# The section ahead of the list in written order: w by two queues, the path's flag by a product with ones, the powers in a weights' buffer, and 14 dummy products on TensorE

## The chip, the cores and the metric

The kernel runs on one core of a Trainium2 chip. A time is the device time of one execution, in microseconds (us). The kernel before was run 9 times: the median is 514.84 us. One further execution was recorded by the hardware profiler; every duration below comes from that one. Engines are named as in the profile: PE is TensorE's matmul side (PEld its weight loads), DVE is VectorE, ACT is ScalarE, POOL is GpSimd and SP is SyncE, which here only issues DMA transfers.

## What is computed

The kernel computes a linear attention with a decaying state, and a feed-forward block on its output, all in float32 (the four weights come as float64 words and are converted in the kernel). B = 4, H = 8, S = 768, D = 48; d_ff = 1024.

```python
for t in range(S):
    kt, vt, rt = (k[:, :, t], v[:, :, t], r[:, :, t])
    cur = np.einsum('bhd,bhe->bhde', u[None] * kt, vt)
    y[:, :, t] = np.einsum('bhd,bhde->bhe', rt, state + cur)
    state = w[None, :, :, None] * state + np.einsum('bhd,bhe->bhde', kt, vt)
x = np.ascontiguousarray(y.transpose(0, 2, 1, 3)).reshape(B * S, H * D)
a = x @ w1
b = x @ w2
out = (a * b @ w3) @ w_out
```

## The kernel before

**Units and the list.** A unit is one chunk of 128 tokens of one batch entry: 6 chunks by 4 entries, 24 units, numbered n. Almost all work is given by a list written out by hand, ORDER, of words such as `d.0` or `a.0.3.2`. `listed()` (line 745) runs through it under `manual_schedule`, so each of PE, ACT, DVE and SP does its instructions in the order of the list. The words that matter here:

- `kr.n`, `v.n` (`load`, line 197): load k and r, or v, of unit n, on SP. k and r go to `krin`, three buffers by n mod 3; v to `vnat`.
- `W.i` (`fetch`, line 218): load weights piece i on SP into `raws[i % 3]`. `M.i`, `N.i`, `H.i`, `L.i`, `Q.i` (lines 327 to 357) convert it on ACT, DVE, DVE, ACT and DVE.
- `d.n`, `e.n`, `f.n` (lines 399 to 408, DVE): r times k into the tile `ruk`, times u (the tile `ub`), and the sum by head. `g.n` (line 410, ACT) places it on diagonals.
- `k.n` (`scale`, line 388, DVE): k and r times the powers of w (`pn`), into `krs`.
- `U.n` (line 498, PE): products for the state. `T.n`, `R.n` (line 436, PE): transposes of `krs`. `A.n` (line 508), `S.n` (line 597) and `V.n` (line 616): the attention's products on PE. `i.n`, `j.n` (line 515, DVE): the state. `m.n` (line 539, DVE): the mask.
- `a`, `b`, `c`, `u` (lines 646 to 663): the products with w1 and w2; `G`, `K`, `F`, `X` fold w3 and w_out into one matrix; `P`, `E`, `D` are the last product and the stores.

The order of the list isn't planned at run time: an instruction goes when it is at the head of its engine and its inputs and its buffer are there.

**The section ahead of the list** (lines 149 to 278) isn't under `manual_schedule`. It does these things:

- POOL makes the identity and the masks and clears the pads of buffers (lines 156 to 191). ACT warms its table with one activation (line 183).
- SP loads w as one row (`wrow`, line 227), w as two columns of 48 partitions (`wucol`, line 229), k and r of unit 0, weights piece 0, u (`ub`, line 232), v of unit 0, k and r of unit 1, weights piece 1 and v of unit 1, in this order (lines 225 to 237).
- DVE finds the smallest and the largest w from `wrow` and writes `flag`, one integer that says whether all of w lies within W_LOW = 0.6 and W_HIGH = 1.6 (lines 240 to 245).
- DVE makes the powers of w: limits it (line 252), squares it six times (line 254), takes reciprocals (line 255) and doubles its way up to 64 positions and their inverses in a tile `both` of its own (lines 258 to 269), and copies each half to its second half (line 271). PE transposes the 8 blocks (line 274) and ACT copies the two results to `pn_in` (line 275).
- Each engine loads `flag` (`values_load`, line 277) and takes the branch to `program(True)` or `program(False)` (line 835). With these inputs it is `program(True)`, the list; `program(False)` is a general path that isn't run.

The tile `both` is freed at the end of that section, and tiles of the list, `ruk` among them, are allotted from the room that it leaves.

Of the kernel before, what the change touches and what calls it, by code (L numbers as in the profile page):

```python
# [23 lines left out]
M.1 h.1 j.0 S.0 t.1 d.2 R.1 k.2 m.0 r.1 R.2 kr.5 e.2 U.1 N.1 r.2 f.2 A.1 M.2 H.1 T.2 i.1 L.1 m.1 V.0 d.3 p.1 W.4 Q.1
v.3 Y.0 t.2 j.1 S.1 g.2 N.2 A.2 k.3 V.1 H.2 R.3 kr.6 Y.1 U.2 m.2 M.3 v.4 T.3 N.3 L.2 a.0.0.0 k.4 r.3 W.5 i.2 a.0.1.0
H.3 p.2 c.0.0.0 e.3 L.3 R.4 j.2 S.2 f.3 M.4 W.6 U.3 Q.3 b.0.0.0 o.4 h.3 c.0.1.0 i.3 t.3 V.2 d.4 p.3 k.5 kr.7 T.4 Y.2
e.4 A.3 v.5 r.4 x.5 S.3 t.4 b.0.1.0 m.3 o.5 y.5 j.3 M.5 V.3 u.0.0.0 u.0.1.0 U.4 f.4 Y.3 v.6 A.4 Q.2 g.4 a.0.0.1 k.6
N.5 b.0.0.1 M.6 N.6 m.4 c.0.0.1 H.6 a.0.1.1 z.5 u.0.0.1 L.6 H.5 b.0.1.1 c.0.1.1 x.6 W.9 L.5 a.0.2.2 u.0.1.1 y.6 i.4
W.8 l.5 Q.6 p.4 d.5 a.0.3.2 Q.5 c.0.2.2 kr.8 j.4 N.4 e.5 S.4 H.4 c.0.3.2 M.8 z.6 U.5 f.5 M.9 V.4 N.8 d.6 L.4 A.5 i.5
kr.9 b.0.2.2 Y.4 h.5 o.6 e.6 W.7 p.5 m.5 v.7 l.6 Q.4 b.0.3.2 j.5 u.0.2.2 N.9 k.7 U.6 f.6 A.6 x.7 g.6 S.5 k.8 y.7 V.5  # L30
d.7 M.7 a.0.4.2 m.6 v.8 kr.10 o.7 e.7 u.0.3.2 Y.5 f.7 z.7 x.8 b.0.4.2 c.0.4.2 d.8 y.8 h.7 kr.11 e.8 i.6 a.0.5.2 f.8
p.6 u.0.4.2 l.7 d.9 j.6 b.0.5.2 c.0.5.2 e.9 H.8 f.9 L.8 H.9 W.11 d.10 L.9 A.7 Q.8 W.12 U.7 u.0.5.2 a.0.6.2 N.7 i.7 H.7
p.7 k.9 L.7 a.0.7.2 j.7 kr.12 c.0.6.2 x.9 W.10 Q.9 y.9 S.6 Q.7 c.0.7.2 z.8 o.8 V.6 m.7 e.10 b.0.6.2 Y.6 g.8 v.9 N.10
N.11 S.7 M.10 f.10 M.11 u.0.6.2 z.9 V.7 o.9 H.10 b.0.7.2 l.8 d.11 Y.7 H.11 v.10 L.10 e.11 L.11 Q.10 W.13 g.9 Q.11 W.14
a.1.0.2 N.12 u.0.7.2 M.12 f.11 H.12 M.13 a.1.1.2 d.12 L.12 N.13 e.12 c.1.0.2 W.15 Q.12 M.14 H.13 N.14 L.13 b.1.0.2
H.14 c.1.1.2 W.16 Q.13 L.14 Q.14 W.17 M.15 N.15 b.1.1.2 H.15 u.1.0.2 L.15 Q.15 W.18 M.16 N.16 A.8 H.16 u.1.1.2 a.1.2.2
L.16 m.8 l.9 W.19 N.17 M.17 Q.16 H.17 M.18 b.1.2.2 N.18 c.1.2.2 H.18 L.17 L.18 Q.17 W.20 M.19 Q.18 W.21 G.0.0 N.19
G.0.1 K.0.0 u.1.2.2 U.8 H.19 a.1.3.2 K.0.1 i.8 L.19 k.10 p.8 W.22 M.20 N.20 kr.13 x.10 F.0 c.1.3.2 H.20 M.21 y.10 j.8
L.20 Q.19 W.23 M.22 Q.20 N.21 N.22 H.21 H.22 L.21 b.1.3.2 X.0 Q.21 W.24 L.22 Q.22 W.25 M.23 N.23 A.9 u.1.3.2 U.9 H.23
S.8 i.9 L.23 z.10 V.8 k.11 o.10 a.1.4.2 g.10 N.24 x.11 v.11 kr.14 Q.23 Y.8 m.9 y.11 b.1.4.2 p.9 W.26 N.25 f.12 c.1.4.2  # L40
j.9 l.10 d.13 e.13 S.9 u.1.4.2 o.11 A.10 z.11 a.1.5.2 m.10 a.1.6.2 c.1.5.2 l.11 a.1.7.2 c.1.6.2 b.1.5.2 V.9 u.1.5.2
U.10 c.1.7.2 v.12 G.1.0 i.10 Y.9 G.1.1 g.11 k.12 b.1.6.2 x.12 kr.15 p.10 f.13 y.12 K.1.0 d.14 b.1.7.2 M.24 j.10 M.25
e.14 u.1.6.2 K.1.1 H.24 S.10 H.25 L.24 z.12 A.11 u.1.7.2 o.12 U.11 Q.24 L.25 V.10 m.11 W.28 G.2.0 k.13 g.12 W.27 G.2.1
v.13 F.1 i.11 kr.16 Q.25 p.11 f.14 N.26 Y.10 j.11 l.12 d.15 K.2.0 x.13 K.2.1 e.15 y.13 N.27 G.3.0 X.1 U.12 S.11 k.14
o.13 V.11 i.12 kr.17 A.12 Y.11 x.14 G.3.1 v.14 g.13 a.2.0.2 z.13 m.12 K.3.0 f.15 y.14 p.12 d.16 G.4.0 K.3.1 e.16
b.2.0.2 j.12 K.4.0 c.2.0.2 l.13 U.13 u.2.0.2 S.12 k.15 z.14 o.14 V.12 i.13 A.13 Y.12 x.15 G.4.1 g.14 v.15 F.2 m.13
y.15 kr.18 K.4.1 f.16 l.14 d.17 M.26 e.17 M.27 H.26 p.13 H.27 L.26 j.13 S.13 L.27 W.29 Q.26 M.28 W.30 V.13 Q.27 o.15
z.15 N.28 A.14 Y.13 H.28 U.14 X.2 m.14 G.5.0 L.28 v.16 G.5.1 i.14 g.15 F.3 W.31 Q.28 N.29 k.16 M.29 f.17 kr.19 p.14
H.29 j.14 L.29 x.16 l.15 Q.29 S.14 y.16 K.5.0 N.30 d.18 X.3 F.4 K.5.1 N.31 e.18 o.16 z.16 G.6.0 X.4 G.6.1 K.6.0 F.5
M.30 K.6.1 H.30 M.31 L.30 H.31 Q.30 L.31 s.1.2.0 Q.31 s.1.2.1 F.6 s.1.0.0 X.5 s.1.2.3 s.1.1.0 s.1.3.0 s.1.1.2 s.1.3.1  # L50
s.1.1.1 s.1.3.3 s.1.3.2 s.1.0.1 s.1.0.2 s.1.0.3 s.1.2.2 G.7.0 X.6 s.1.1.3 U.15 K.7.0 G.7.1 i.15 P.0.0.0 K.7.1 k.17
p.15 F.7 x.17 kr.20 j.15 y.17 A.15 X.7 s.0.1.0 V.14 s.0.0.0 E.0.0.0 l.16 B.0 P.0.1.0 Y.14 v.17 s.0.0.1 g.16 m.15
a.2.1.2 s.0.0.3 B.1 E.0.1.0 f.18 B.2 a.2.2.2 c.2.1.2 B.3 s.0.1.2 s.0.0.2 s.0.2.0 b.2.1.2 d.19 c.2.2.2 s.0.2.2 s.0.2.1
s.0.1.1 s.0.2.3 s.0.3.0 b.2.2.2 s.0.1.3 s.0.3.1 u.2.1.2 s.0.3.3 e.19 s.0.3.2 P.0.0.2 u.2.2.2 P.0.1.2 E.0.0.2 P.0.0.3
E.0.1.2 P.0.0.4 E.0.0.3 P.0.1.3 E.0.0.4 P.0.0.5 E.0.1.3 P.0.1.5 E.0.0.6 E.0.0.5 D.0.0.0 P.0.1.4 E.0.1.6 A.16 E.0.1.4
U.16 E.0.1.5 m.16 D.0.1.0 P.0.0.6 i.16 k.18 p.16 P.0.0.1 j.16 kr.21 S.15 x.18 z.17 o.17 V.15 E.0.0.1 E.0.0.7 U.17 Y.15
a.2.3.2 i.17 g.17 y.18 v.18 k.19 D.0.0.1 kr.22 p.17 f.19 a.2.4.2 l.17 d.20 j.17 c.2.3.2 x.19 e.20 y.19 P.0.1.1 c.2.4.2
# [34 lines left out]
def kernel(  # L92
# [139 lines left out]
    nc.sync.dma_start(out=ub.rearrange("t h d -> t (h d)"),  # L232
                      in_=u.rearrange("h d -> (h d)").rearrange("(o n) -> o n", o=1).to_broadcast([P, DM]))
# [12 lines left out]


    pn_in = const.tile([C, 2, H, PAD], F32)
    with tc.tile_pool(name="once", bufs=1) as once, tc.tile_pool(name="psW", bufs=2, space=PSUM) as psW:
# [9 lines left out]
        nc.vector.memset(both[:, 0, :, HT:HT + 1], 1.0)  # L259
        nc.vector.tensor_copy(out=both[:, 1, :, HT:HT + 1], in_=wn_in[:, 0, NP:2 * NP, :])  # L260
        bf = both.rearrange("x g p t -> x (g p) t")
        for l in range(LEVELS):
# [4 lines left out]
            nc.vector.tensor_mul(bf[:, :, HT - 2 * n + 1:HT - n + 1] if n < HT else bf[:, :, 0:1],
                                 bf[:, :, HT - n + 1:HT + 1] if n < HT else bf[:, :, HT:HT + 1],
                                 wn_in[:, l, 0:2 * NP, :].to_broadcast([P, 2 * NP, n if n < HT else 1]))
        for g in range(2):  # L270
            nc.vector.tensor_copy(out=both[:, g, :, T:], in_=both[:, g, :, :T])
            ps = psW.tile([P, NP, C], F32, tag="w", name=f"ps_p{g}")
            for p in range(NP):
                nc.tensor.transpose(ps[:, p, :], both[:, g, p, :], ident)
# [594 lines left out]
```

## Time and profile before

| | |
|---|---|
| median of 9 runs | 514.84 us (513.56 to 517.12) |
| the profiled execution: its own time | 516.05 us |
| its span, first to last instruction | 514.2 us |
| granted TensorE clock, mean | 0.99 |
| busy: PE, PEld | 492.1 us (96%), 323.5 us (63%) |
| busy: DVE, ACT, POOL | 278.1 us (54%), 183.7 us (36%), 6.1 us (1%) |
| moved by DMA | 52.72 MB, mean 103 GB/s |
| landing after issue, median: k, r, v | 3.9, 4.3, 4.0 us |
| landing after issue, median: weights piece of 768 KB | 6.1 us |

How to read the profile's views: the page cuts the span into 40 slices of 12.9 us and gives the busy share of each engine in tenths, and the granted clock of TensorE in tenths of full speed. The chain of work that ended last is followed back from the last instruction, at each step to what released it; its lines give start, length and what ran. The timeline gives start, length, engine, line, operation and tiles, and in brackets how long the engine had been idle and what released it. For SP, a line is the issue of a DMA, and its length is the time that the issue took, not the transfer. A table of stages gives, for each stretch, the busy time of each engine, the granted clock and the DMA engines' share.

### The profile page before, as it was taken

The page shows a single profiled execution, that of the slowest core. Times are in us where ns is not written, and L with a number is a line of the kernel's source. Part 1 is how long each engine was busy: PE and PEld are TensorE (multiplying, and loading weights), DVE is VectorE, ACT ScalarE, POOL GpSimd, SP SyncE. Part 2 cuts the span into 40 slices and gives each one's busy share as a digit, 9 for nine tenths or more (in the row PEclk, how much of TensorE's full clock was granted, in tenths as well). Part 3 has the DMA queues.
Part 4 walks back from the last instruction along what each step waited for, and adds up shares of the span by engine and source line. Part 5 has one row for each costly group of instructions (what it writes and reads, how often), then busy time and mean ns, then how long its engine had stood idle before and what let it go on. Part 6 is the DMA issues. An engine that isn't in the chain of part 4 may idle for free.

```text
span 514.2 us, 12195 instructions
## 1 busy us (share of the span) xinstructions
PE 492.1 (96%) x5192; PEld 323.5 (63%) x5192; DVE 278.1 (54%) x587; ACT 183.7 (36%) x455; POOL 6.1 (1%) x23
## 2 busy tenths in 40 slices
PE   1889999999999899999999999999999999999996
...
PEclk9969999999999999999999999999999999999999
DMA  7988796668547781302601301230050100000001
GB/s 171 231 221 243 184 245 189 182 222 247 157 104 199 188 228 31 78 1 63 170 32 57 83 0 46 64 89 22 0 144 28 48 2 0 15 17 17 1 17 67
DMA packets 96865, 52.72 MB, mean 103 GB/s; under 512 B 77729, under 2 KB 88226, under 8 KB 96802
## 3 DMA queue, kind: packets, MB, share of 16 engines
...
q8 instruction: 43, 0.70, 0.6%
...
## 4 chain that ended last, share of the span: by engine, by line
PE 87%; DMA 6%; DVE 4%; issue 1%; ACT 1%; SPq 0%; DVEq 0%; ACTq 0%
PE ps_a L652 23%; PE ps_b L652 22%; PE ps_w L380 7%; PE ps_y L626 3%; PE ps_s4b L709 3%; PE ps_a11b L709 3%; PE ps_a22t L709 3%; PE ps_s2t L709 3%; PE ps_a12b L709 3%; PE ps_s1t L709 3%; PE ps_s3t L709 3%; PE ps_y L612 3%; PE ps_a L512 3%; PE ps_a L505 2%; DMA raw<-in_moe_w_dram 2%; DMA krin<-in_r_dram 1%
## 5 line engine op out<-in xcount | busy, mean ns | idle before, releaser
L652 PE MATMUL ps_a<-xT,w 128*128 128x512 f32 (+1 forms) x300 | 132.4, 585 | 0.0
L652 PE MATMUL ps_b<-xT,w 128*128 128x512 f32 (+1 forms) x300 | 130.9, 577 | 0.0
L652 PEld LDWEIGHTS ps_b<-xT,w 128*128 128x128 f32 x300 | 56.2, 190 | 62.0 <-issue 57.6
L663 DVE TENSOR_TENSOR abt<-ps_b,a 128x512 f32<-128x512 f32 (+1 forms) x50 | 33.3, 667 | 109.9 <-PE ps_b L652 109.9
L652 PEld LDWEIGHTS ps_a<-xT,w 128*128 128x128 f32 x300 | 56.1, 193 | 57.1 <-issue 53.6
L658 ACT COPY a<-ps_a 128x512 f32<-128x512 f32 (+1 forms) x50 | 28.3, 567 | 132.6 <-PE ps_a L652 128.0
L537 ACT COPY wide<-st 64x192 f32<-64x192 f32 x88 | 30.6, 347 | 59.4 <-DVE st L529 27.6
L380 PE MATMUL ps_w<-wo,w3T 128*128 128x384 f32 x128 | 42.5, 487 | 0.0
L419 ACT ACTIVATE AT<-same,dg 128x64 f32<-128x64 f32 x160 | 40.4, 336 | 5.5 <-DVE dg L408 3.0
L380 PEld LDWEIGHTS ps_w<-wo,w3T 128*128 128x128 f32 x128 | 23.9, 190 | 15.7 <-ACT wide L537 0.2
L354 ACT ACTIVATE t<-raw 128x512 uint32<-128x512 uint32 (+2 forms) x32 | 22.4, 706 | 7.7 <-DVE w3n L350 5.1
L626 PE MATMUL ps_y<-AT,vnat 64*64 64x64 f32 x1152 | 23.3, 226 | 1.2 <-issue 1.2
L540 DVE COPY_PREDICATED AT<-later,ps_a 128x512 f32<-128x512 int32 x24 | 17.5, 730 | 11.1 <-PE ps_a L505 7.0
L392 DVE TENSOR_TENSOR krs<-krin,pn_in 128x768 f32<-128x768 f32 x24 | 22.8, 949 | 0.1
L626 PEld LDWEIGHTS ps_y<-AT,vnat 64*64 64x64 f32 x1152 | 20.0, 138 | 4.4 <-issue 2.7
L505 PE MATMUL ps_a<-vnat,krs 64*64 64x48 f32 x704 | 17.2, 227 | 5.5 <-DVE krs L392 3.3
L612 PEld LDWEIGHTS ps_y<-tt,wide 128*32 128x32 f32 x1056 | 16.1, 111 | 9.5 <-issue 5.7
L461 DVE STREAM_TRANSPOSE tr<-krs 128x768 f32<-128x768 f32 x19 | 18.5, 973 | 4.9 <-DMA scratch<-tr 4.7
L505 PEld LDWEIGHTS ps_a<-vnat,krs 64*64 64x64 f32 x704 | 14.7, 142 | 9.9 <-issue 7.9
L612 PE MATMUL ps_y<-tt,wide 128*32 128x64 f32 x1056 | 20.0, 223 | 0.7 <-ACT xT L634 0.7
L512 PEld LDWEIGHTS ps_a<-tt,kT 64*64 64x64 f32 x768 | 15.0, 141 | 8.9 <-issue 4.6
L512 PE MATMUL ps_a<-tt,kT 64*64 64x64 f32 x768 | 18.2, 231 | 2.1 <-DVE st L528 1.1
...
## 6 DMA issues: line engine op xcount, KB each, us to landing
...
```

The source lines that it names most:

```text
L380: nc.tensor.matmul(ps, lhsT=w3T[j][:, kc, :], rhs=wo[kc], start=(kc == 0), stop=(kc == KF - 1))
L392: nc.vector.tensor_mul(krs[n % NS][:, :, :, :D], kr, pn[:, :, :, :D])
L419: nc.scalar.activation(out=AT[n][:, i, p, :], in_=same, func=COPY, scale=dg[n][:, h:h + 1])
L505: nc.tensor.matmul(added(n)[rows(i), a, p, :], lhsT=kk[rows(a), 2 * p + i, :], rhs=vnat[n % NV][rows(a), 2 * p + i, 0:D], start=True, stop ...
L512: nc.tensor.matmul(upper(n)[rows(a), i, p, :], lhsT=kT[n][rows(i), p, rows(a)], rhs=rT[n][rows(i), p, 2 * a:2 * a + 2], start=True, stop=True)
L537: nc.scalar.copy(out=wide[a][n % 2][rows(i), :, i * D:(i + 1) * D], in_=st[units[n][1]][rows(i)])
L612: nc.tensor.matmul(yt[n][g * Q:(g + 1) * Q, a, q, :], lhsT=wide[a][n % 2][:, p, j * Q:(j + 1) * Q], rhs=rw[:, p, 2 * a:2 * a + 2] if fast ...
L626: nc.tensor.matmul(yt[n][rows(g), a, q, :], lhsT=vv[rows(a), x:x + PAD], rhs=AT[n][rows(a), h % 2, h // 2, :], start=(a, g) not in seen, s ...
L652: nc.tensor.matmul(ps, lhsT=(w1 if x == "a" else w2)[:, z, q, js], rhs=xT[c][:, q, ts], start=(q == 0), stop=(q == KM - 1))
L658: nc.scalar.copy(out=a, in_=ps)
L663: nc.vector.tensor_mul(abt[c, j][:, parts_of_tokens[part]], factor["b", c, j, part], factor["sa", c, j, part])
L709: nc.tensor.matmul(ps, lhsT=of[:, m * C:(m + 1) * C], rhs=w34[:, KH * (x == 1) + j, :DH] if x < 2 else made[b][:, j, :], start=(j == 0), s ...
```

## The change

The change touches the section ahead of the list; the list's steps and their order stay as they are, but for `kr.n`, which is written as `kk.n rr.n` (load k, then load r).

- `wrow` and the two reductions are gone. The two halves of `wucol` are loaded by two queues, SP's and ACT's.
- v of unit 0 is loaded ahead of u.
- The section runs under `manual_schedule` for PE, ACT, DVE and SP, so in written order on each.
- PE does 14 products of a tile of ones with itself, whose result isn't used.
- The tile `both` lies in `raws[2]`, the buffer of weights pieces 2, 5, 8 and so on.
- The flag: w is compared with its limited value (1 where they differ), a product with a column of ones sums over the partitions, DVE adds up the four sums, and the flag is 1 where the total is 0.
- The second of the two copies to the upper half goes to ACT.
- The list gets names that it doesn't use (`ka`, `kb`, `Z`), and `scale` an argument that is left at its default.

```diff
-    wucol = const.tile([P, NP, 1], F32)
-    nc.vector.memset(wucol, 1.0)
-    warm = const.tile([1, 1], F32)
-    nc.vector.memset(warm, 0.0)
-    nc.scalar.activation(out=warm, in_=warm, func=ABS)
...
-    wrow = const.tile([1, DM], F32)
     ub = const.tile([P, H, D], F32)
-    nc.sync.dma_start(out=wrow, in_=w.rearrange("h d -> (h d)").rearrange("(o n) -> o n", o=1))
-    for i in range(2):
-        nc.sync.dma_start(out=wucol[i * PAD:i * PAD + D], in_=w.rearrange("(p i) (d o) -> i d p o", i=2, o=1)[i])
-    load(0, "kr")
-    fetch(0)
-    nc.sync.dma_start(out=ub.rearrange("t h d -> t (h d)"),
-                      in_=u.rearrange("h d -> (h d)").rearrange("(o n) -> o n", o=1).to_broadcast([P, DM]))
-    load(0, "v")
-    load(1, "kr")
-    fetch(1)
-    load(1, "v")
-    ends = const.tile([1, 3], F32)
...
-    nc.vector.tensor_reduce(ends[:, 0:1], wrow, AX.X, ALU.min)
-    nc.vector.tensor_reduce(ends[:, 1:2], wrow, AX.X, ALU.max)
-    nc.vector.tensor_scalar(ends[:, 2:3], ends[:, 0:1], W_LOW, None, ALU.is_ge)
-    nc.vector.scalar_tensor_tensor(flag, ends[:, 1:2], W_HIGH, ends[:, 2:3], ALU.is_le, ALU.mult)
...
+    with tc.manual_schedule(engines={PE, ACT, DVE, SP}), tc.tile_pool(name="psW", bufs=2, space=PSUM) as psW:
+        nc.vector.memset(wucol, 1.0)
+        for i, queue in enumerate((nc.sync, nc.scalar)):
+            queue.dma_start(out=wucol[i * PAD:i * PAD + D], in_=w.rearrange("(p i) (d o) -> i d p o", i=2, o=1)[i])
+        load(0, "kr")
+        fetch(0)
+        load(0, "v")
+        nc.sync.dma_start(out=ub.rearrange("t h d -> t (h d)"),
+                          in_=u.rearrange("h d -> (h d)").rearrange("(o n) -> o n", o=1).to_broadcast([P, DM]))
+        load(1, "kr")
+        fetch(1)
+        load(1, "v")
+
+        busy = pn_in[:, 0].rearrange("t h d -> t (h d)")[:, :C]
+        nc.vector.memset(busy, 1.0)
+        ps_busy = psW.tile([P, C], F32, tag="busy", bufs=1, name="ps_busy")
+
+        def keep_busy(times):
+            for _ in range(times):
+                nc.tensor.matmul(ps_busy, lhsT=busy, rhs=busy, start=True, stop=True)
+
+        keep_busy(14)
+        nc.vector.memset(warm, 0.0)
+        nc.scalar.activation(out=warm, in_=warm, func=ABS)
+
+        both = raws[2].bitcast(F32)[:, :2 * NP * C].rearrange("x (g p t) -> x g p t", g=2, p=NP)
+        bf = both.rearrange("x g p t -> x (g p) t")
+        nc.vector.memset(outs[:, NP:NP + 1], 1.0)
+        nc.vector.memset(both[:, 0, :, HT:HT + 1], 1.0)
         nc.vector.tensor_scalar(wn_in[:, 0, 0:NP, :], wucol, W_LOW, W_HIGH, ALU.max, ALU.min)
         for l in range(LEVELS):
             nc.vector.tensor_mul(wn_in[:, l + 1, 0:NP, :], wn_in[:, l, 0:NP, :], wn_in[:, l, 0:NP, :])
+            if l == 0:
+
+                nc.vector.tensor_tensor(outs[:, 0:NP], wn_in[:, 0, 0:NP, 0], wucol[:, :, 0], ALU.not_equal)
+                ps_out = psW.tile([1, NP], F32, tag="out", bufs=1, name="ps_out")
+                nc.tensor.matmul(ps_out, lhsT=outs[:, NP:NP + 1], rhs=outs[:, 0:NP], start=True, stop=True)
...
-        both = once.tile([P, 2, NP, C], F32)
...
+        nc.vector.tensor_copy(out=both[:, 0, :, T:], in_=both[:, 0, :, :T])
+        nc.scalar.copy(out=both[:, 1, :, T:], in_=both[:, 1, :, :T])
+        nc.vector.tensor_reduce(outs[0:1, NP + 1:], ps_out, AX.X, ALU.add)
+        nc.vector.tensor_scalar(flag, outs[0:1, NP + 1:], 0.0, None, ALU.is_equal)
         for g in range(2):
-            nc.vector.tensor_copy(out=both[:, g, :, T:], in_=both[:, g, :, :T])
```

In ORDER, only `kr.2` to `kr.23` change, each into two words:

```diff
-kr.2 v.2 d.0 W.2 N.0 e.0 f.0 M.0 k.0 g.0 H.0 U.0 kr.3 d.1 T.0 k.1 L.0 R.0 e.1 kr.4 t.0 i.0 f.1 r.0 T.1 W.3 Q.0 p.0 A.0
+kk.2 rr.2 v.2 d.0 W.2 N.0 e.0 f.0 M.0 k.0 g.0 H.0 U.0 kk.3 rr.3 d.1 T.0 k.1 L.0 R.0 e.1 kk.4 rr.4 t.0 i.0 f.1 r.0 T.1
```

More of the change, by code (lines that the diff above doesn't have):

```diff
@@ L22 @@
 ORDER = """
-kr.2 v.2 d.0 W.2 N.0 e.0 f.0 M.0 k.0 g.0 H.0 U.0 kr.3 d.1 T.0 k.1 L.0 R.0 e.1 kr.4 t.0 i.0 f.1 r.0 T.1 W.3 Q.0 p.0 A.0
[L24 to L57, printed above, removed]
+kk.2 rr.2 v.2 d.0 W.2 N.0 e.0 f.0 M.0 k.0 g.0 H.0 U.0 kk.3 rr.3 d.1 T.0 k.1 L.0 R.0 e.1 kk.4 rr.4 t.0 i.0 f.1 r.0 T.1
@@ new lines @@
+W.3 Q.0 p.0 A.0 M.1 h.1 j.0 S.0 t.1 d.2 R.1 k.2 m.0 r.1 R.2 kk.5 rr.5 e.2 U.1 N.1 r.2 f.2 A.1 M.2 H.1 T.2 i.1 L.1 m.1
+V.0 d.3 p.1 W.4 Q.1 v.3 Y.0 t.2 j.1 S.1 g.2 N.2 A.2 k.3 V.1 H.2 R.3 kk.6 rr.6 Y.1 U.2 m.2 M.3 v.4 T.3 N.3 L.2 a.0.0.0
+k.4 r.3 W.5 i.2 a.0.1.0 H.3 p.2 c.0.0.0 e.3 L.3 R.4 j.2 S.2 f.3 M.4 W.6 U.3 Q.3 b.0.0.0 o.4 h.3 c.0.1.0 i.3 t.3 V.2
+d.4 p.3 k.5 kk.7 rr.7 T.4 Y.2 e.4 A.3 v.5 r.4 x.5 S.3 t.4 b.0.1.0 m.3 o.5 y.5 j.3 M.5 V.3 u.0.0.0 u.0.1.0 U.4 f.4 Y.3
+v.6 A.4 Q.2 g.4 a.0.0.1 k.6 N.5 b.0.0.1 M.6 N.6 m.4 c.0.0.1 H.6 a.0.1.1 z.5 u.0.0.1 L.6 H.5 b.0.1.1 c.0.1.1 x.6 W.9
@@ new lines @@
+L.5 a.0.2.2 u.0.1.1 y.6 i.4 W.8 l.5 Q.6 p.4 d.5 a.0.3.2 Q.5 c.0.2.2 kk.8 rr.8 j.4 N.4 e.5 S.4 H.4 c.0.3.2 M.8 z.6 U.5
+f.5 M.9 V.4 N.8 d.6 L.4 A.5 i.5 kk.9 rr.9 b.0.2.2 Y.4 h.5 o.6 e.6 W.7 p.5 m.5 v.7 l.6 Q.4 b.0.3.2 j.5 u.0.2.2 N.9 k.7
+U.6 f.6 A.6 x.7 g.6 S.5 k.8 y.7 V.5 d.7 M.7 a.0.4.2 m.6 v.8 kk.10 rr.10 o.7 e.7 u.0.3.2 Y.5 f.7 z.7 x.8 b.0.4.2
+c.0.4.2 d.8 y.8 h.7 kk.11 rr.11 e.8 i.6 a.0.5.2 f.8 p.6 u.0.4.2 l.7 d.9 j.6 b.0.5.2 c.0.5.2 e.9 H.8 f.9 L.8 H.9 W.11
+d.10 L.9 A.7 Q.8 W.12 U.7 u.0.5.2 a.0.6.2 N.7 i.7 H.7 p.7 k.9 L.7 a.0.7.2 j.7 kk.12 rr.12 c.0.6.2 x.9 W.10 Q.9 y.9 S.6
@@ new lines @@
+Q.7 c.0.7.2 z.8 o.8 V.6 m.7 e.10 b.0.6.2 Y.6 g.8 v.9 N.10 N.11 S.7 M.10 f.10 M.11 u.0.6.2 z.9 V.7 o.9 H.10 b.0.7.2 l.8
+d.11 Y.7 H.11 v.10 L.10 e.11 L.11 Q.10 W.13 g.9 Q.11 W.14 a.1.0.2 N.12 u.0.7.2 M.12 f.11 H.12 M.13 a.1.1.2 d.12 L.12
+N.13 e.12 c.1.0.2 W.15 Q.12 M.14 H.13 N.14 L.13 b.1.0.2 H.14 c.1.1.2 W.16 Q.13 L.14 Q.14 W.17 M.15 N.15 b.1.1.2 H.15
+u.1.0.2 L.15 Q.15 W.18 M.16 N.16 A.8 H.16 u.1.1.2 a.1.2.2 L.16 m.8 l.9 W.19 N.17 M.17 Q.16 H.17 M.18 b.1.2.2 N.18
+c.1.2.2 H.18 L.17 L.18 Q.17 W.20 M.19 Q.18 W.21 G.0.0 N.19 G.0.1 K.0.0 u.1.2.2 U.8 H.19 a.1.3.2 K.0.1 i.8 L.19 k.10
@@ new lines @@
+p.8 W.22 M.20 N.20 kk.13 rr.13 x.10 F.0 c.1.3.2 H.20 M.21 y.10 j.8 L.20 Q.19 W.23 M.22 Q.20 N.21 N.22 H.21 H.22 L.21
+b.1.3.2 X.0 Q.21 W.24 L.22 Q.22 W.25 M.23 N.23 A.9 u.1.3.2 U.9 H.23 S.8 i.9 L.23 z.10 V.8 k.11 o.10 a.1.4.2 g.10 N.24
+x.11 v.11 kk.14 rr.14 Q.23 Y.8 m.9 y.11 b.1.4.2 p.9 W.26 N.25 f.12 c.1.4.2 j.9 l.10 d.13 e.13 S.9 u.1.4.2 o.11 A.10
+z.11 a.1.5.2 m.10 a.1.6.2 c.1.5.2 l.11 a.1.7.2 c.1.6.2 b.1.5.2 V.9 u.1.5.2 U.10 c.1.7.2 v.12 G.1.0 i.10 Y.9 G.1.1 g.11
+k.12 b.1.6.2 x.12 kk.15 rr.15 p.10 f.13 y.12 K.1.0 d.14 b.1.7.2 M.24 j.10 M.25 e.14 u.1.6.2 K.1.1 H.24 S.10 H.25 L.24
@@ new lines @@
+z.12 A.11 u.1.7.2 o.12 U.11 Q.24 L.25 V.10 m.11 W.28 G.2.0 k.13 g.12 W.27 G.2.1 v.13 F.1 i.11 kk.16 rr.16 Q.25 p.11
+f.14 N.26 Y.10 j.11 l.12 d.15 K.2.0 x.13 K.2.1 e.15 y.13 N.27 G.3.0 X.1 U.12 S.11 k.14 o.13 V.11 i.12 kk.17 rr.17 A.12
+Y.11 x.14 G.3.1 v.14 g.13 a.2.0.2 z.13 m.12 K.3.0 f.15 y.14 p.12 d.16 G.4.0 K.3.1 e.16 b.2.0.2 j.12 K.4.0 c.2.0.2 l.13
+U.13 u.2.0.2 S.12 k.15 z.14 o.14 V.12 i.13 A.13 Y.12 x.15 G.4.1 g.14 v.15 F.2 m.13 y.15 kk.18 rr.18 K.4.1 f.16 l.14
+d.17 M.26 e.17 M.27 H.26 p.13 H.27 L.26 j.13 S.13 L.27 W.29 Q.26 M.28 W.30 V.13 Q.27 o.15 z.15 N.28 A.14 Y.13 H.28
@@ new lines @@
+U.14 X.2 m.14 G.5.0 L.28 v.16 G.5.1 i.14 g.15 F.3 W.31 Q.28 N.29 k.16 M.29 f.17 kk.19 rr.19 p.14 H.29 j.14 L.29 x.16
+l.15 Q.29 S.14 y.16 K.5.0 N.30 d.18 X.3 F.4 K.5.1 N.31 e.18 o.16 z.16 G.6.0 X.4 G.6.1 K.6.0 F.5 M.30 K.6.1 H.30 M.31
+L.30 H.31 Q.30 L.31 s.1.2.0 Q.31 s.1.2.1 F.6 s.1.0.0 X.5 s.1.2.3 s.1.1.0 s.1.3.0 s.1.1.2 s.1.3.1 s.1.1.1 s.1.3.3
+s.1.3.2 s.1.0.1 s.1.0.2 s.1.0.3 s.1.2.2 G.7.0 X.6 s.1.1.3 U.15 K.7.0 G.7.1 i.15 P.0.0.0 K.7.1 k.17 p.15 F.7 x.17 kk.20
+rr.20 j.15 y.17 A.15 X.7 s.0.1.0 V.14 s.0.0.0 E.0.0.0 l.16 B.0 P.0.1.0 Y.14 v.17 s.0.0.1 g.16 m.15 a.2.1.2 s.0.0.3 B.1
@@ new lines @@
+E.0.1.0 f.18 B.2 a.2.2.2 c.2.1.2 B.3 s.0.1.2 s.0.0.2 s.0.2.0 b.2.1.2 d.19 c.2.2.2 s.0.2.2 s.0.2.1 s.0.1.1 s.0.2.3
+s.0.3.0 b.2.2.2 s.0.1.3 s.0.3.1 u.2.1.2 s.0.3.3 e.19 s.0.3.2 P.0.0.2 u.2.2.2 P.0.1.2 E.0.0.2 P.0.0.3 E.0.1.2 P.0.0.4
+E.0.0.3 P.0.1.3 E.0.0.4 P.0.0.5 E.0.1.3 P.0.1.5 E.0.0.6 E.0.0.5 D.0.0.0 P.0.1.4 E.0.1.6 A.16 E.0.1.4 U.16 E.0.1.5 m.16
+D.0.1.0 P.0.0.6 i.16 k.18 p.16 P.0.0.1 j.16 kk.21 rr.21 S.15 x.18 z.17 o.17 V.15 E.0.0.1 E.0.0.7 U.17 Y.15 a.2.3.2
+i.17 g.17 y.18 v.18 k.19 D.0.0.1 kk.22 rr.22 p.17 f.19 a.2.4.2 l.17 d.20 j.17 c.2.3.2 x.19 e.20 y.19 P.0.1.1 c.2.4.2
@@ L61 @@
 P.2.1.0 E.1.1.5 E.1.1.6 D.1.1.0 P.1.1.6 A.17 E.1.1.7 S.16 D.1.1.1 E.2.1.0 m.17 z.18 o.18 V.16 U.18 g.18 a.2.5.2 i.18
-v.19 k.20 p.18 f.20 kr.23 x.20 l.18 a.2.6.2 c.2.5.2 j.18 y.20 d.21 e.21 b.2.5.2 c.2.6.2 a.2.7.2 u.2.5.2 s.2.1.0
+v.19 k.20 p.18 f.20 kk.23 rr.23 x.20 l.18 a.2.6.2 c.2.5.2 j.18 y.20 d.21 e.21 b.2.5.2 c.2.6.2 a.2.7.2 u.2.5.2 s.2.1.0
 s.2.1.2 s.2.1.1 s.2.1.3 b.2.6.2 c.2.7.2 b.2.7.2 u.2.6.2 s.2.2.0 s.2.2.1 s.2.2.2 s.2.2.3 a.3.0.2 Y.16 u.2.7.2 s.2.3.0
@@ L234 @@
-    load(0, "v")
-    load(1, "kr")
-    fetch(1)
-    load(1, "v")
-    ends = const.tile([1, 3], F32)
-    flag = const.tile([1, 1], I32)
-    nc.vector.tensor_reduce(ends[:, 0:1], wrow, AX.X, ALU.min)
-    nc.vector.tensor_reduce(ends[:, 1:2], wrow, AX.X, ALU.max)
-    nc.vector.tensor_scalar(ends[:, 2:3], ends[:, 0:1], W_LOW, None, ALU.is_ge)
-    nc.vector.scalar_tensor_tensor(flag, ends[:, 1:2], W_HIGH, ends[:, 2:3], ALU.is_le, ALU.mult)
-    pn_in = const.tile([C, 2, H, PAD], F32)
-    with tc.tile_pool(name="once", bufs=1) as once, tc.tile_pool(name="psW", bufs=2, space=PSUM) as psW:
-        wn_in = const.tile([P, LEVELS + 1, 3 * NP, 1], F32)
+    wucol = const.tile([P, NP, 1], F32)
@@ new lines @@
+    pn_in = const.tile([C, 2, H, PAD], F32)
+    wn_in = const.tile([P, LEVELS + 1, 3 * NP, 1], F32)
+    outs = const.tile([P, NP + 2], F32)
+    flag = const.tile([1, 1], I32)
+    warm = const.tile([1, 1], F32)
+    with tc.manual_schedule(engines={PE, ACT, DVE, SP}), tc.tile_pool(name="psW", bufs=2, space=PSUM) as psW:
[23 more added lines that the diff above has]
+        nc.vector.memset(both[:, 0, :, HT:HT + 1], 1.0)
```

13 lines of the change are left out of this document (8 added, 5 removed).

## The prediction

> **What bounds the kernel now.** I read the page's slices first, then the chain of work that ended last for the first 60 us, then the timeline of the first 13 us with the DMA landings of single tiles, then a table of stages with the granted clock. From the page:
>
> ```profile
> span 514.2 us, 12195 instructions
> PE   1889999999999899999999999999999999999996
> ...
> PEclk9969999999999999999999999999999999999999
> DMA  7988796668547781302601301230050100000001
> ```
>
> PE is busy 492.1 of 514.2 us. The 22 us that it is idle lie mostly in the first three slices (12.9 us each); from 38 us on it runs its list almost without a gap (73.5 of 74 us up to 112). So an edit of the section ahead of the list can only be worth what it moves the start of that dense list. In those slices the DMA engines are the busiest thing on the core, and in slice three the granted clock falls to 0.6. The chain, from its answer for 0 to 60 us:
>
> ```profile
> 1.61 1.89 DMA wucol<-in_w_dram
> ...
> 7.60 1.95 PE ps_p L274 x8
> ...
> 9.64 0.37 DVE ruk L401
> ...
> 15.99 0.88 DVE w L357
> 16.86 0.22 SPq L204
> 17.08 0.04 issue
> 17.13 7.60 DMA krin<-in_r_dram
> ...
> 24.85 0.13 DVE ruk L401
> 25.32 0.95 DVE w L357
> ...
> 26.69 1.13 PE ps_a L512 x32
> ```
>
> The chain has three legs: the section ahead (w lands, DVE makes the powers, PE transposes them), DVE's first units, and the load of r for unit 3, for which DVE waits 0.89 us at 24.85 (step d.3). From 26.69 PE is the chain. The join at 17 us I don't believe: the r.3 load writes a buffer that Q.0 (L357) does not touch. What SP really waits for is room. From the timeline:
>
> ```profile
> 3.98 0.48 SPq L232 DMA_DIRECT2D ub<-in_u_dram  x1
> 4.51 0.43 SPq L204 DMA_DIRECT2D vnat<-in_v_dram  x1
> ...
> 5.61 4.08 SPq L204 DMA_DIRECT2D krin<-in_r_dram  x1
> ...
> 9.64 0.56 DVE L401 TENSOR_TENSOR ruk<-krin 128x384 f32<-128x384 f32 x1 [1.98 <-PE ps_p L274]
> ...
> 10.58 0.55 DVE L404 TENSOR_TENSOR ruk<-ruk,ub 128x384 f32<-128x384 f32 x1
> ```
>
> The r.1 load writes a fresh buffer, yet its issue takes 4.08 us and ends at 9.69, just after the first weights piece landed (issued 3.19, 6.2 us to landing: 9.4). The same shows at 12.17 (2.76 us) and 18.80 (3.05 us). SP's issues run back to back from 0.81 to 24 us save one gap of 0.67 us at the branch (11.09 to 11.76). So the early stage is a stream of transfers in SP's order, paced by the DMA engines, and r.3 lands at 24.72 because the stream began when it began.
>
> **The change, part by part.**
>
> *Removed DMA and second queue (SP).* The first k load was issued at 2.08, behind one wrow issue (0.35, pitch 0.40) and two wucol issues (0.43 and 0.35, pitch 0.44). After, only one wucol issue stands ahead, and it waits for DVE's memset of wucol (0.88 to 0.94 before, so about 1.0): k.0 goes out at 1.0 + 0.43 = 1.43. The whole stream moves up by 0.65 us. Bounds: 0.4 (SP starts later than 1.0) to 0.83 (it keeps 0.81). A rule bears on this: the Trainium skill, "DMA: Bandwidth & Descriptors", section "Issuing engines are not separate DMA queues", says that starting DMAs from several engines saves only the sequencer's time to issue, usually little beside the transfer. By it the second queue is worth 0.35 and the lost wrow 0.40, and against a median landing of 4 to 6 us that would be noise. The rows say otherwise here: the stream behind is unbroken, so what is saved ahead of it is not hidden. Sum by the rule alone 0.0 to 0.35, by the rows 0.65; I take the rows.
>
> *The w half on ACT's queue.* ACT's first work was a table load, 0.80 to 2.08. If the DMA goes ahead of it, w lands at about 1.0 + 1.9 = 2.9; if behind, at 4.0, against 3.49 now. So the powers start 0.6 us earlier or 0.5 later.
>
> *The powers (DVE).* From L252's start to the end of the last product is 3.54 us (3.60 to 7.14). A compare is put in, priced as L254 (0.20 pitch): 3.74. The two 128x256 copies (0.49 together) become one on DVE and one on ACT: 0.29. Then a tiny reduce and compare for the flag, at L244's 0.13 to L254's 0.17 each: 0.3. Removed: two reductions over wrow (0.54 and 0.53) and two tiny operations, all but 0.04 of which lay in the wait for w. Flag ready at 3.0 + 3.74 + 0.29 + 0.3 = 7.3 (8.4 with w late), against 4.0 now.
>
> *The later flag is the added wait.* Behind it on each engine stands the whole list. SP gets there at 11.09 − 0.65 = 10.4, ACT and PE after the table of powers at about 9: all after it is written. DVE pays it itself. SP's gap at the branch prices load and branch at 0.6, so DVE starts d.0 at about 8.0 (9.0). Now it starts d.0 at 9.64, because the buffer of the powers, which the list's tile reuses, was read by PE until 9.54. With the powers in a weights' buffer this wait of 1.98 is gone: 0.6 to 1.6 us gained on DVE.
>
> *What is late next.* DVE runs d.0, N.0, e.0, f.0, k.0. N.0 needs weights piece 0, which lands at 9.4 − 0.65 = 8.75. e.0 needs ub. ub is now issued behind v.0, so it takes v.0's place in the stream: v.0 landed at 4.51 + 6.1 = 10.6 and ub at 3.98 + 6.0 = 9.98; ub now lands at 10.6 − 0.65 = 9.96. So e.0 starts at 10.05 instead of 10.58, and k.0 at 11.1 instead of 11.64: of up to 1.6 us, 0.53 is left. v.0 lands earlier and nothing waited for it.
>
> *14 dummy products (PE).* At the transposes' pitch of 1.94/8 = 0.24 they take 3.4 us, from about 1.2 to 4.6, while PE was idle until 7.6; the one-row product needs powers that aren't there before 4. Cost nothing. What they may bring: eight transposes took 1.94 us, a transpose in the cold stage 0.43 (four in 1.11 at 13.88), later 0.28 (four in 0.63 at 20.32). Warm they would take 1.26, so the table of powers would be ready up to 0.7 earlier. It is ready at 10.17 now; after, at 9.0 to 9.6 (10.7 at worst), while k.0 can't go before 11.1: worth 0. A rule speaks against the dummies lasting: "TensorE: Matmul & The Clock Gate", Part 1, says that the array goes to full clock after about 3.4 us of sustained work and falls back after such a window of idleness, in windows that run free of the program's start. By it 3.4 us of products fill a window only by luck, and PE's idle stretch from 9 to U.0 at 12.3 cools it again. The rows agree on the fall:
>
> ```profile
> 24.00:26.00 2.00, 1.00 (x38) 0.72 (x37) 1.15 (x2) 1.79 (x5) 0.00 (x0) 0.96 0.70 145
> 26.00:28.00 2.00, 1.31 (x49) 1.34 (x52) 1.97 (x5) 1.77 (x8) 0.00 (x0) 0.50 0.96 309
> ...
> 36.00:38.00 2.00, 2.00 (x12) 1.74 (x11) 1.97 (x5) 1.80 (x5) 0.00 (x0) 0.98 0.64 116
> ```
>
> (columns after the length: PE, PEld, DVE, ACT, POOL busy, clock, DMA share, GB/s). The clock is halved from 25.9 to 36.1, after windows in which PE worked half the time. The fall comes long after the dummies; I give them 0.
>
> *Powers in raws[2].* The third weights load (W.2, issued 15.72) must now wait for the transposes' reads, done by 9: a cover of 6 us, cost 0. Without that cover k.3 and r.3 behind it on SP would wait. *The k and r loads named apart* are the same two issues in the same order: 0. *PSUM for the dummies and the flag*: its readers are done before U.0, 0.
>
> *Sum.* Stream −0.65, DVE −0.53; at d.3 the stream binds, with 0.89 us of DVE slack, so the d.3 to PE leg moves up by 0.65. From there the list is PE's, and its own DMA waits (87.7, 93.1, 100.3, 153.8) hang on PE's and ACT's releases, so they move along. Against the profiled execution: 516.05 − 0.65 = 515.4. That execution stood 1.2 above the median; on the median 514.84 − 0.65 = **514.2**.
>
> **The rivals.** *The half-clock stretch (faster).* From 26.7 to 37.8 PE is the chain, and chain pieces there cost more than the same pieces at full clock: A 1.13 against 0.62, V 1.28 against 0.86, R and T 1.04 against 0.59 each, U 1.47 against 0.61, 12 products 3.54 against 2.98: together 3.25 us in 10.2 us. The nine runs spread by 3.56, which is that size: some executions likely lack it. If the earlier, closer work of PE keeps the clock up in most executions, the median goes to the best run less the shift, 513.56 − 0.65 = 512.9. For: PE is denser at the start. Against: the fall follows a thin stretch at 22 to 26 that nothing touches. 0.20.
>
> *DVE's start decides (faster).* If the transfers aren't the bound, ub lands early enough, and all of d.0's 1.6 passes on: 513.2. For: the chain as printed runs through DVE to 16.86. Against: DVE's 0.89 wait for r.3, and ub's landing. 0.20.
>
> *A longer half-clock stretch (slower).* PE warms early, so between 12 and 26 it finishes sooner and idles more, and the clock falls a window or more earlier in the chain's stage. At 3.25/10.2 = 0.32 per us the loss passes 0.3% once the stretch is (1.54 + 0.65)/0.32 = 6.9 us longer; twice as long gives 514.2 + 3.25 = 517.4. 0.14.
>
> *The change doesn't do what it says.* SP's first issue waits and ACT's w lands at 4.0: the stream gains 0.4 at most, time 514.5 to 514.8. 0.06, inside "same".
>
> **How the numbers follow.** 0.3% is 1.54 us, about what a measurement of this kernel can tell from no change. Likeliest case 0.40 at 514.2, its own range 513.4 to 515.0, same; with the case of no effect, same 0.46. Faster 0.40 from the two rivals (512.9 and 513.2), slower 0.14. The range reaches below both faster cases by the 0.7 that a median of such runs may move, 512.2, and up to 516.0, leaving out most of the slower case.
>
> **What would show it.** The first k load issued at 1.4; r.3 landed at 24.1; d.0 at 8 to 9 and e.0 behind ub at 10; k.0 at 11.1; PE idle between 9 and 12.3; the half clock again near 26 to 36. If k.0 starts much before 11, or r.3 lands elsewhere than 0.65 earlier, the reading of the stream is wrong. If all early steps come as said and the end moves by over 1.5 us, the clock was the cause, and the clock column at 25 to 38 must differ.

## The result, and the profile after

The changed kernel takes 510.05 us (median of 16 runs, 508.35 to 514.28), the kernel before 514.69 (53 runs, 511.31 to 518.75): a ratio of 0.9922, 95% interval 0.9904 to 0.994. That is 4.6 us gained where 0.65 was forecast, and outside the range. The page of the changed kernel:

```profile
span 510.6 us, 12255 instructions
PE   5689999999999999999999999999999999999996
...
PEclk9889999999999999999999999999999999999999
DMA  8898877668449591303503201230060100000001
```

PE's first slices are filled by the dummies, the clock shows 0.8 in slices two and three in place of 0.9 and 0.6, and 60 instructions more stand in the program. The section ahead of the list went as forecast, or a little better. From the timeline:

```profile
1.41 0.43 SPq L200 DMA_DIRECT2D krin<-in_k_dram  x1
...
8.23 0.56 DVE L413 TENSOR_TENSOR ruk<-krin 128x384 f32<-128x384 f32 x1 [0.85 <-DVE flag L282]
...
9.61 0.56 DVE L416 TENSOR_TENSOR ruk<-ruk,ub 128x384 f32<-128x384 f32 x1 [0.35 <-DMA ub<-in_u_dram]
...
10.68 0.95 DVE L404 TENSOR_TENSOR krs<-krin,pn_in 128x768 f32<-128x768 f32 x1
```

k of unit 0 goes out at 1.41 (forecast 1.43); d.0 starts at 8.23 (8.0); e.0 waits for u until 9.6 (10.05) and k.0 starts at 10.68 (11.1). The first state product, U.0, is 0.96 us earlier than before. That isn't 3.6 us, by which the spans differ. So I set PE's steps of the two traces side by side. The changed kernel's steps run 0.4 to 1.9 us ahead up to U.2, 1.5 at U.2 itself, and at the next step, T.3, the lead is 3.7. PE's timeline of the kernel before at that place:

```profile
29.03 1.11 PE L439 MATMUL ps_rT<-ident,krs 128*128 128x128 f32 x4
30.07 0.45 PE L505 MATMUL ps_a<-vnat,krs 64*64 64x48 f32 x5
32.15 1.09 PE L505 MATMUL ps_a<-vnat,krs 64*64 64x48 f32 x27 [1.62 <-issue]
33.17 1.11 PE L439 MATMUL ps_kT<-ident,krs 128*128 128x128 f32 x4
```

and of the changed kernel:

```profile
27.50 1.11 PE L451 MATMUL ps_rT<-ident,krs 128*128 128x128 f32 x4
28.55 0.97 PE L517 MATMUL ps_a<-vnat,krs 64*64 64x48 f32 x32
29.45 0.66 PE L451 MATMUL ps_kT<-ident,krs 128*128 128x128 f32 x4
29.95 2.76 PE L664 MATMUL ps_a<-xT,w 128*128 128x256 f32 x12
```

The second line of the first fence and the third are one step, U.2, of 32 products. After five of them PE stops for 1.62 us, and "issue" says that nothing in the profile released it: the profile shows no data and no buffer that was missing. In the changed kernel the same 32 run through in 0.97. The kernel before has three more such stops, in V.0 (0.87 at 24.26, and 0.30 at 45.80 in another pairs step) and at 173.64 (1.01): 3.8 us in all. The changed kernel has 0.2.

### The profile page after: what moved, and what is told of

Its sections match the earlier page's. It is cut to its first block, busy times and chain, and to the rows that moved or that the text cites. A ratio compares the mean times of both kernels' runs of the same rounds, so it can differ in the third digit from the quotient of the medians.

```text
span 510.6 us, 12255 instructions
## 1 busy us (share of the span) xinstructions
PE 493.6 (97%) x5222; PEld 324.4 (64%) x5222; DVE 277.3 (54%) x587; ACT 183.3 (36%) x456; POOL 6.0 (1%) x23
## 4 chain that ended last, share of the span: by engine, by line
PE 85%; DMA 8%; SPq 2%; ACT 2%; DVE 1%; issue 1%; ACTq 0%; DVEq 0%
PE ps_b L664 22%; PE ps_a L664 22%; PE ps_w L392 7%; PE ps_y L638 3%; PE ps_s4b L721 3%; PE ps_y L624 3%; PE ps_a11b L721 3%; PE ps_a22t L721 3%; PE ps_a12b L721 3%; PE ps_s1t L721 3%; PE ps_s3t L721 3%; PE ps_s2t L721 3%; PE ps_a L517 3%; DMA raw<-in_moe_w_dram 2%; DMA tt<-scratch 2%; PE ps_a L524 2%
## 5 line engine op out<-in xcount | busy, mean ns | idle before, releaser
L392 PEld LDWEIGHTS ps_w<-wo,w3T 128*128 128x128 f32 x128 | 23.9, 190 | 15.7 <-ACT wide L549 0.2
L490 ACT COPY kT<-tt 128x512 f32<-128x512 f32 x19 | 11.7, 617 | 21.2 <-DMA tt<-scratch 19.6
L359 DVE TENSOR_SCALAR t<-raw 128x512 uint32<-128x512 uint32 (+2 forms) x32 | 13.9, 437 | 9.8 <-DMA raw<-in_moe_w_dram 6.8
```

Source lines behind the costliest of these rows:

```text
L392: nc.tensor.matmul(ps, lhsT=w3T[j][:, kc, :], rhs=wo[kc], start=(kc == 0), stop=(kc == KF - 1))
```

## The experiments

Each theory is an answer to the question where the 4.6 us come from. Theory A: the earlier start, which shifts PE's work against the stretches of half clock. Theory B: the dummies warm PE, so that its clock is up earlier. Theory C (the powers' new buffer) and theory D (the stops belong to the kernel before, not to one execution) came with the first four kernels, and theory E, below, after them. Each kernel was timed beside the kernel before on the same chip; ratios are to that.

**Without the dummies** (`keep_busy(14)` to `keep_busy(0)`).

> The changed kernel without its 14 dummy products. Theory A (the earlier start): units start 0.96 us earlier because u and the first k and r land earlier, and the first state product at 11.9 instead of 12.8 fills a whole window of the clock, so PE is at full speed at 15.6 instead of 19.0; the dummies only make the table of powers ready early, which has 1 us of slack. It expects the time of the changed kernel, 510.0, within 0.8, and full clock again at about 15.6. Theory B (the dummies warm PE): without them most of the gain goes, 512.5 to 514.5, and the clock comes at 19.

513.72 us, ratio 0.9971 (0.9949 to 0.9992). Most of the gain is gone, so A falls: the clock is at full speed from 16.0, about where A had it, and the time is not what A had. What is left to the rest of the change is 1.5 us (0.4 to 2.6). The stop in U.2 is back: 2.64 us, after four products.

**The kernel before with the dummies alone.**

```diff
+        busy = pn_in[:, 0].rearrange("t h d -> t (h d)")[:, :C]
+        nc.vector.memset(busy, 1.0)
+        ps_busy = psW.tile([P, C], F32, tag="busy", bufs=1, name="ps_busy")
+        for _ in range(14):
+            nc.tensor.matmul(ps_busy, lhsT=busy, rhs=busy, start=True, stop=True)
         wn_in = const.tile([P, LEVELS + 1, 3 * NP, 1], F32)
```

> The kernel before with nothing but the 14 dummy products ahead of the transposes. Theory A: units start as before but for the transposes (1.9 us to 1.1), for which the first r times k waits: up to 0.8 earlier on DVE, of which u's landing leaves little; 513.5 to 514.7. Theory B: 510.5 to 512.

511.51 us, ratio 0.9933 (0.9905 to 0.9962). The dummies do most of it by themselves, as B had it, and there is no stop in V.0 or U.2. One of 0.78 stands in a later pairs step, at 42.48.

**The powers in a tile of their own** (`both` from a pool of one buffer, closed ahead of the list).

> The changed kernel with the powers in a tile of their own, freed ahead of the list, in place of the weights' buffer: the first r times k must wait for the transposes again. Theory A: transposes end at 8.4, the wait for u ends at 9.6, so nothing changes: 510.0 within 0.8. A theory C (the weights' buffer is what DVE gains by) expects 511 or more.

509.65 us, ratio 0.9899 (0.987 to 0.9928): nothing is lost. C falls; the wait for u stands behind this one, as the prediction said.

**The kernel before, once more.**

> The kernel before, unchanged, for a second trace of it. Theory A: the clock reaches full speed at 19.0 again and the state products of unit 2 stand in the half-clock stretch. Theory D (PE's stall of 1.62 us within the state products of unit 2, and one of 1.0 at 172, belong to the kernel before and not to one execution): both stalls are there again at the same places. If they are not, they are chance and the profiled pair overstates the gain. Time 514.7 within 0.6.

514.16 us, ratio 0.9991 (0.9973 to 1.0009). The products take their short times from 16.2 on this time, not from 19.0, and the half-clock stretch is 29.9 to 36.7 in place of 25.8 to 36.1: the clock's changes are not tied to a place in the program. The stops in V.0 and U.2, though, are where they were, as D had it, and so is the one of 1.0 (at 173.30 now); the one of 0.30 at 45.80 is gone:

```profile
23.49 0.46 PE L626 MATMUL ps_y<-AT,vnat 64*64 64x64 f32 x14 [0.79 <-issue]
...
27.80 0.32 PE L505 MATMUL ps_a<-vnat,krs 64*64 64x48 f32 x5
31.04 1.09 PE L505 MATMUL ps_a<-vnat,krs 64*64 64x48 f32 x27 [2.92 <-issue]
```

In both traces V.0 stops with 14 of its 48 products left and U.2 after five. Between the two places lie 14 + 24 (S.1) + 32 (A.2) + 48 (V.1) + 4 (R.3) + 5 = 127 products, 254 instructions with their weight loads and 256 with the two waits that PE's stream has there. The page lists one queue of instruction transfers that fits:

```profile
q8 instruction: 43, 0.70, 0.6%
q14 instruction: 20, 0.16, 0.1%
```

43 transfers of 0.70 MB are some 16.3 KB each. PE has 5192 products and as many weight loads, 10384 instructions, and 10384/256 is 41. The Trainium skill, "Runtime: NRT & Kernel Launch", section "Instruction fetch mechanics", says that an engine's instructions are refilled in blocks of 16 KiB, 256 instructions, and that crossing a block's end is mostly hidden. The size agrees with the counts here. "Mostly hidden" does not: here a crossing cost up to 3.6 us. So theory E: PE stops where a block ends and the next has not landed; the 28 products in the trace that the 14 dummies make (each stands there twice) move all these places to 28 products earlier in the list.

**As many instructions without the work** (14 products of one column in the changed kernel).

```diff
-        keep_busy(14)
+        def keep_short(times):
+            for _ in range(times):
+                nc.tensor.matmul(ps_busy[0:1, 0:1], lhsT=busy[:, 0:1], rhs=busy[:, 0:1], start=True, stop=True)
+
+        keep_short(14)
```

> The changed kernel, its 14 dummy products cut to one weight column and one moving column: as many PE instructions, hardly any work. Theory E (instruction refill): the traces of the three kernels without dummies stall within the pairs step V.0 and again 127 products on, in U.2, which is 254 instructions with the weight loads, while an instruction transfer is under way; the 28 products of the dummies move these places back to where PE has just idled. It expects no stall in U.2, and 509.5 to 511. Theory B (warmth): without the work there is no warmth, 513 to 514.5, and the stall in U.2 is there.

510.09 us, ratio 0.9911 (0.9883 to 0.9939): the whole gain. Its PE timeline:

```profile
1.15 0.84 PE L255 MATMUL ps_busy<-pn_in 128*1 128x1 f32 x28 [1.15 <-DVE raw L264]
...
7.28 1.94 PE L291 MATMUL ps_p<-ident,raw 128*128 128x128 f32 x8 [3.12 <-DVE outs L286]
...
27.16 0.74 PE L456 MATMUL ps_rT<-ident,krs 128*128 128x128 f32 x4
27.83 0.68 PE L522 MATMUL ps_a<-vnat,krs 64*64 64x48 f32 x32
```

The short products are over in 0.84 us, the transposes take 1.94 us again, as in the kernel before (1.06 behind the real dummies), and yet U.2 runs through. B falls.

**Four products of 512 columns** (`keep_busy(4)` on a tile of 512 columns: as much work in 8 products of the trace).

> The changed kernel with 4 dummy products of 512 columns in place of 14 of 128: about as long on PE (some 5 us), but 8 products in the trace in place of 28. Theory E: the refill's places move by 8 products only, from the 5th of U.2 to the last of V.1 or to R.3, where PE has no slack either; a stall of 1 us or more stays at 26 to 29 us, and the time is 512 to 514. Theory B: 509.5 to 511.

511.33 us, ratio 0.9931 (0.9906 to 0.9957). That lies between the two expectations, and E missed its detail: the trace has no stop at 26 to 29. PE had just waited 2.25 us for ACT ahead of S.1, and the block was there. This one doesn't tell E from B.

**A whole period** (14 dummies, and 50 products of one column after the transposes).

> The changed kernel with 50 products of one column (100 in the trace) after the transposes of the powers, where PE idles for 3.5 us: with the 28 of the dummies that makes 128, a whole period of 256 instructions, so that the places of the refill are back where they were without dummies, while the array is as warm or warmer. Theory E: the stall in U.2 is back, 512.5 to 514. Theory B: 509.5 to 511.

512.18 us, ratio 0.9959 (0.993 to 0.9989), and the stop is back at its place, after four products of U.2, as without dummies:

```profile
26.78 0.32 PE L519 MATMUL ps_a<-vnat,krs 64*64 64x48 f32 x4
28.17 0.67 PE L519 MATMUL ps_a<-vnat,krs 64*64 64x48 f32 x28 [1.07 <-issue]
```

So is the other, of 0.97 us at 169, after 11 products of an A step (13 in the kernel before, at 173.6). The dummies stand in this kernel as in the changed one, the transposes behind them take 1.07 us (1.06 there), and the clock is full at the stop. This is E, and not B. The stop is shorter than without dummies, and the time a little under what E gave.

**Units later** (three memsets on DVE between the flag and the list).

```diff
+        pad = raws[2].bitcast(F32)[:, 2 * NP * C:]
+        for _ in range(3):
+            nc.vector.memset(pad, 0.0)
```

> The changed kernel with three memsets (1.5 us on DVE) between the flag and the list, so that the first r times k starts at 9.7 and the first state product at about 12.7, as in the kernel before; no transfer is touched. If the stream of transfers binds, as the prediction had it, nothing is lost: 510.0 within 0.8. If DVE's start decides, 510.7 to 511.2.

511.54 us, ratio 0.994 (0.9915 to 0.9964). U.0 starts at 12.64, 0.76 later. The median is 1.5 above the changed kernel's, but the intervals of the two ratios overlap, so whether the start costs that can't be said. In the one trace of it the lateness is down to 0.13 us by 32.7, and U.3 starts 1.25 us earlier than in the changed kernel (33.80 for 35.05).

**The kernel before with the short products alone.**

> The kernel before with nothing but 14 products of one column (28 in the trace) ahead of the transposes: no warmth, no earlier transfer, no other buffer; only the places of PE's instructions move by 28 products. Theory E (refill): no stall in V.0 and U.2, time 511 to 512.5 (as with the dummies alone, 511.5). Theory B (warmth): 514 to 515, with the stalls.

510.46 us, ratio 0.9914 (0.9884 to 0.9944), and no stop at all in its trace. V.0 and U.2 run through:

```profile
22.49 0.93 PE L631 MATMUL ps_y<-AT,vnat 64*64 64x64 f32 x48
...
30.47 0.68 PE L510 MATMUL ps_a<-vnat,krs 64*64 64x48 f32 x32
```

Nothing else of the change is in this kernel, U.0 starts at 13.2, later than before, and it gains what the whole change gains.

**Other numbers of short products** in the changed kernel: 7, then 32.

> The changed kernel with 7 products of one column in place of the 14 dummies: the places of the refill are 14 products earlier than without any, at the 19th of V.0 and the 42nd of V.1. Theory E: PE comes to V.1 from a wait for ACT and has done some 100 products by then, so a short stall may show there; 510 to 512.5. Theory B: 513 to 514.5.

> The changed kernel with 32 products of one column: half a period (64 products), so that the refill falls into A.1 and A.2 (about the 5th and the 24th). Theory E: A.2 comes right behind PE's wait for ACT, so the refill has landed, and there is no stall in V.0 or U.2; 509 to 511.5. Theory B: 513 to 514.5.

With 7: 513.9 us, ratio 0.9972 (0.9939 to 1.0004), not told from no change: B's range, not E's. With 32: 516.22, ratio 1.0036 (1.001 to 1.0062), slower than the kernel before, where E expected a gain; it lies outside both ranges. The places were E's, their price was not. Of 7:

```profile
21.63 0.56 PE L643 MATMUL ps_y<-AT,vnat 64*64 64x64 f32 x19
22.42 0.68 PE L643 MATMUL ps_y<-AT,vnat 64*64 64x64 f32 x29 [0.23 <-issue]
...
25.57 0.86 PE L643 MATMUL ps_y<-AT,vnat 64*64 64x64 f32 x42
30.07 0.49 PE L643 MATMUL ps_y<-AT,vnat 64*64 64x64 f32 x6 [3.64 <-issue]
```

The stops are after the 19th of V.0 and the 42nd of V.1, the places that were expected, and the second costs 3.64 us instead of "a short stall". Of 32:

```profile
66.52 0.34 PE L643 MATMUL ps_y<-AT,vnat 64*64 64x64 f32 x6 [2.38 <-issue]
```

There is no stop in V.0 or U.2, but later ones, at 42.35 (1.31), 66.52 (2.38), 161.92 (0.76) and 181.16 (1.12), which I had not looked for: 5.6 us in all.

**u ahead of v** with 14 short products.

> The changed kernel with 14 products of one column, and u loaded ahead of v of unit 0 as in the kernel before. In the changed kernel DVE's step e.0 waits 0.35 us for u, at 9.6; with u first it needn't, and the first state product goes some 0.4 us earlier if the table of powers allows it. If DVE's start decides the early stage: 509.3 to 509.9. If the stream of transfers does, as the prediction had it: 510.1 within 0.8, as with u second.

510.91 us, ratio 0.9941 (0.9915 to 0.9968), against 0.9911 (0.9883 to 0.9939) with u second: k.0 starts at 10.22, and nothing is gained.

All the kernels, by the sum of PE's stops that "issue" ended after 13 us, one trace each:

| kernel | stops, us | ratio |
|---|---|---|
| before; its second trace | 3.8; 4.7 | 1; 0.9991 |
| 32 short products | 5.6 | 1.0036 |
| 7 short products | 4.9 | 0.9972 |
| no dummies | 2.9 | 0.9971 |
| a whole period | 2.1 | 0.9959 |
| dummies alone; wide dummies | 0.8; 0.6 | 0.9933; 0.9931 |
| own tile; late units | 0.4; 0.3 | 0.9899; 0.994 |
| changed; u first | 0.2; 0.2 | 0.9922; 0.9941 |
| 14 short products; the same in the kernel before | 0; 0 | 0.9911; 0.9914 |

Every kernel with at most 0.8 us of stops has a ratio of 0.9941 or less, and every one with 2 us or more 0.9959 or more. Within each group the order isn't kept (7 short products have more stops than the kernel before and a lower ratio): the stops are those of one trace, the ratio that of many executions, and executions of one kernel differ (511.31 to 518.75 for the kernel before).

**All the stops on one count.** Counting every record of PE in a trace from its start (weight loads, products and waits), all 22 "issue" stops of 0.25 us or more after 13 us, in 10 of the 14 traces, come at the 194th or 195th record of a period of 256, whatever was inserted and whichever step runs there. The other four traces have no such stop. And the transfers of q8 fit one to one: at the k-th of these places PE had the k-th transfer behind it, begun at least 2.25 us earlier, at all of the first 40 places in all 14 traces (560), and at the 22 stops 2.31 to 2.78 us earlier.

Where the stop comes from also shows in time. The second instruction transfer, which is the one ahead of the stop in U.2, in the DMA view of the kernel before, for 29.6 to 29.8 us:

```profile
q1 hardware_dynamic: 132, 0.02, 61.3%
q8 instruction: 1, 0.02, 31.6%
```

31.6% of 16 engines for 0.2 us is 1.0 us of one engine, counted where it begins. PE goes on at 32.15, 2.55 us after that slice's start. In four further traces the same distance is 2.64 (second trace of before), 2.67 (7 short products), 2.52 (32) and 2.57 (whole period). So PE goes on some 2.5 us after its block's transfer began, 1.5 us more than the transfer's own 1.0; what fills these 1.5 us no view shows.

## Why the prediction was wrong

*The step that failed* is "14 dummy products (PE)": "Cost nothing", "What they may bring" only warmth, "I give them 0". For warmth that was right: without the work the gain stays (510.09), and the clock that the dummies bring does fall again, as the prediction expected (0.53 between 12 and 15 us in the changed kernel, after PE's idle 3.53). But an instruction is also a place in PE's stream. Moved by 28 products, the ends of the second and the third block fall behind waits of PE (for ACT until 24.97, for v until 35.05), in which the block had time to land, and all but 0.2 of 3.8 us of stops are gone. Measured: 0.9914 for the instructions alone in the kernel before, which is 4.4 us by that ratio.

*The stop was there to be seen.* The chain of work for the first 60 us, from which the prediction took its lines, has "30.52 1.62 issue" within PE's step U.2. I left it out of the fence and out of the price of U.2 in the half-clock stretch, took that stretch for the clock's doing alone, and never asked what an "issue" of 1.6 us on the engine that sets the end is.

*The early steps* were right in kind: k.0's load at 1.41, d.0 at 8.2 as soon as the flag allowed, e.0 held by u, k.0 held by e.0 and not by the table of powers. The shift was 0.96 at U.0 in place of 0.53, as u landed at 9.5. The dummies took 5.4 us on PE, not 3.4, since each stands twice in the trace; the flag's product came behind them, at 6.46, and nothing waited for that. The load of r for unit 3 landed at about 23.3, 1.4 earlier and not 0.65.

*That the early shift passes on* isn't shown. Without dummies the rest of the change is worth 1.5 us (0.4 to 2.6); on top of the short products it isn't seen (0.9922 and 0.9914 with overlapping intervals). The two traces say where such a lead goes. ACT waits for weights piece 2 in both; the first line is of the kernel before, the second of the changed one:

```profile
22.13 0.94 ACT L342 ACTIVATE w<-raw 128x768 f32<-128x768 f32 x1 [0.50 <-DMA raw<-in_moe_w_dram]
22.04 0.90 ACT L354 ACTIVATE w<-raw 128x768 f32<-128x768 f32 x1 [2.01 <-DMA raw<-in_moe_w_dram]
```

The piece was issued 0.84 us earlier (14.88 for 15.72) and came 0.09 earlier. PE's S.1 stands behind ACT (3.04 us of waiting, until 24.97), and there the lead is down to 0.41. So the forecast that the whole stream moves up by 0.65 and hands it on to PE's list didn't hold: r of unit 3 came 1.4 earlier, this piece not.

*The closing rule* of the prediction, that the clock must be the cause if the early steps come and the end moves by more, was wrong. The half-clock stretch is shorter (25.8 to 29.2 in place of 25.9 to 36.1), but the whole-period kernel has no half clock after 23 and gains less, and the 14 short products have it from 23.9 to 27.4 and gain as much. What the clock alone is worth here was not isolated.

*What stays open*: what decides when a block's transfer begins. By the count above, the transfer for one place begins near the time when PE passes the place before, in half of the 560 cases between 1.0 us ahead of it and 1.4 after it. Ahead of the stop in U.2 it began 5.4 us after (29.67, PE having passed the end in V.0 at 24.26); for the second block of the changed kernel 0.5 after (21.60, PE at 21.07). Why it was late there, and whether the busy DMA engines are the reason, no run here isolates. So the price of a place can't be worked out beforehand yet; three guesses of it failed here (wide dummies, 7 and 32 short products).
